# A gated linear attention and an MLP on one core: shared-memory work reordered, one cumulative sum per block, w_in in four pieces

## The chip, the core and the metric

The kernel runs on one core of a Trainium2 chip. The core has five instruction streams that run side by side and wait for each other by semaphores: TensorE (PE, matrix products into the accumulator memory PSUM), VectorE (DVE), ScalarE (ACT), GpSimd (POOL) and SyncE (SP), which here only issues data transfers. GpSimd issues transfers too. VectorE, ScalarE and GpSimd work on SBUF, the on-chip memory; VectorE and ScalarE can read PSUM as well. The metric is the device time of one execution in microseconds (us); lower is better.

## The reference: what is computed

```python
f = 1.0 / (1.0 + np.exp(-f_logit))              # q, k, v, f_logit: (4, 8, 768, 48)
for t in range(S):
    state = f[:, :, t, :, None] * state + np.einsum('bhd,bhe->bhde', k[:, :, t], v[:, :, t])
    y[:, :, t] = np.einsum('bhd,bhde->bhe', q[:, :, t], state)
x = y.transpose(0, 2, 1, 3).reshape(3072, 384)
h = x @ w_in                                     # w_in: (384, 2048)
g = 0.5 * (h + np.sqrt(h * h + 4.0))
out = g @ w_out                                  # w_out: (2048, 384)
```

A recurrent attention with a gate per key channel is followed by a two-layer MLP over all 3072 tokens.

## The kernel before

The 3072 tokens are cut into 12 blocks `p` of 256 tokens, three to a batch entry. A block stands on 128 partitions with two neighbouring tokens to a partition, and its two halves of 64 partitions are two chunks of 128 tokens. Within a chunk the recurrence is done as masked matrix products; from chunk to chunk a state of 48x48 per head is carried.

Each block goes through small named pieces. `lf`, `lq`, `lk`, `lv` load the inputs (SyncE). `ex` takes exp(-f) (ScalarE), `ut` adds 1 and gives tile `UT` (line L182), `tt` multiplies the two tokens' gates (L136), `ln` takes the logarithm, tile `s`. `hi` and `lo` split `s` into two 16-bit parts in tile `hl` (L133, L207). `cu` sums `s` over time by TensorE: two triangular matrices `tri`, each times `hi` and `lo` (L221), and small sums over an indicator matrix (L226). `ep` and `ea` are exp of the one sum and of minus the other (ScalarE, L235). `qu`, `ku` multiply q and k by the gates (L136), `qm`, `km` multiply those by `ea`, `ep` into the 16-bit tile `qk` (L136, two instructions each), `vc` casts v. `ge`, `gs`, `gb` are small decay factors. `tp`/`te` transpose `qk` by TensorE for blocks 0 to 3 (L310); `tx` does it by a DMA transpose for the later blocks. `sc` is the score product (L334), `pm` masks it (L341, reads PSUM), `yt` and `yn` give y (L391, L400), `kv`, `ia`, `sa`, `sb` carry the state (L353, L364, L371, L378). `yc` copies y, `xp`/`xe` or a DMA transpose `xx` turn it into tile `xT`.

The MLP of a block is eight pieces `m1` of six products each (L440), eight `sq` (square, ScalarE, L449), four `rt` (square root, ScalarE, L455), eight `gt` (VectorE, L465, reads PSUM), eight `m2` of four products each (L477), two `ev` (copy out) and the stores `st`. `wi0` to `wi7` load and cast w_in in eight pieces of 256 columns, `wo0` to `wo7` w_out, all issued by GpSimd in its own stream.

The order of all pieces is written out by hand in the string `ORDER`, one word each: `ut0.0:P` is piece `ut` of block 0, part 0, on P = GpSimd (D = VectorE, A = ScalarE, S = SyncE, T = TensorE with its PSUM banks behind @). Block 0 is done in two halves of four heads. Each engine runs its pieces strictly in this order, so a piece that waits holds back all behind it on its engine. `TABLE:e` and `TABLE:s` load ScalarE's function tables (exp and log, or square root). `DEPTH` says how many buffers a tile name has.

Of the kernel before, what the change touches and what calls it, by code (L numbers as in the profile page):

```python
# [47 lines left out]
tt7.0:D ln6.0:A lq6.0:S yt3:T@37 sa3:D ln7.0:A st0.01.1:S m2.1.12:T TABLE:s rt2.0:A vc4.0:D km5.0:P ia3.1:T yn3.1:T m2.1.13:T
sb3:D tx4.0:S yc3.0:D m1.2.3:T@2 yc3.1:D xp3.0:T@1 qm5.0:P m1.2.5:T@3 ev1.1:A xe3.0:D tx4.1:S sq2.3:A gt2.1:D m1.2.4:T@7
lv5.0:S rt2.1:A gt2.0:D xp3.1:T@6 m1.2.6:T@1 hi7.0:P xe3.1:D sq2.5:A kv4:T@50 lq7.0:S gt2.2:D hi6.0:P ia4.0:T sq2.4:A qu6.0:P  # L50
m1.2.7:T@6 gt2.3:D rt2.2:A m2.2.10:T@4 st0.01.0:S sa4:D gb5:P gs5:D m2.2.11:T sq2.6:A gt2.5:D ia4.1:T sq2.7:A m1.3.0:T@2
# [559 lines left out]
```

## Time and profile before

| what | value |
|---|---|
| time, median of 3 runs | 220.79 us (220.07 to 221.23) |
| the profiled execution | 221.5 us, of which 219.7 us lie between first and last instruction (the span) |
| PE busy | 183.4 us, 83% of the span |
| DVE busy | 162.9 us, 74% |
| ACT busy | 155.3 us, 71% |
| POOL busy | 118.4 us, 54% |
| mean granted TensorE clock | 0.966 of full speed |

Busy is the time in which an engine runs an instruction; for VectorE and GpSimd that includes time in which an instruction has begun but does not get on. A chain is the sequence of work that ended last, followed back from the end, at each step to what released it. The row groups below are copied from such views.

### The profile page before, as it was taken

The numbers are of one execution on the slowest core, as the hardware profiler recorded it, in microseconds if no ns is written. First come the engines' busy times: TensorE is split into PE (matmuls) and PEld (weight loads), VectorE is DVE, ScalarE is ACT, GpSimd is POOL, SyncE is SP. The second block draws the span as 40 slices with busy tenths as digits, with TensorE's granted clock in tenths as the row PEclk, the third lists the DMA queues.
The fourth block names the chain that finished last, engine by engine and source line by source line (L and its number), as shares of the span: only waits on it lengthen the run. The fifth ranks groups of instructions, "written<-read, shape, count | busy, mean of one in ns | idle before, by whom it ended". The sixth has DMA issues, their size and how long they took to land.

```text
span 219.7 us, 5661 instructions
## 1 busy us (share of the span) xinstructions
PE 183.4 (83%) x2320; PEld 130.2 (59%) x2320; DVE 162.9 (74%) x284; ACT 155.3 (71%) x252; POOL 118.4 (54%) x128
## 2 busy tenths in 40 slices
PE   0348948869589999976995799999989999999991
PEld 0225626646357776745763358678666787777760
DVE  6889685898569999959975976879557875463650
ACT  4633684979747899859994376798848859887920
POOL 6899477299975966889999902939000000000002
PEclk9999996999999999999999658999999999999998
DMA  6999999089980989999969797981991017102204
GB/s 167 267 261 248 215 267 191 8 178 214 250 188 1 206 178 282 182 238 255 174 141 142 151 141 198 184 167 29 186 126 39 0 39 144 38 1 72 75 19 125
DMA packets 82073, 32.87 MB, mean 150 GB/s; under 512 B 73952, under 2 KB 82000, under 8 KB 82048
## 3 DMA queue, kind: packets, MB, share of 16 engines
q1 hardware_dynamic: 76528, 29.07, 65.5%
q0 software_dynamic: 5520, 3.44, 10.5%
q8 instruction: 18, 0.29, 0.5%
q14 instruction: 7, 0.06, 0.1%
HBM read 25.17 MB, written 4.72 MB: 136 GB/s over the span
## 4 chain that ended last, share of the span: by engine, by line
PE 44%; DVE 15%; POOL 12%; ACT 11%; DMA 10%; issue 4%; SPq 2%; POOLq 0%; DVEq 0%
PE ps L440 18%; PE ps L477 18%; POOL UT L182 6%; DMA wout<-in_moe_w_out_dram 4%; ACT r L455 3%; DMA win<-in_moe_w_in_dram 3%; DVE qk L136 3%; DVE UT L136 3%; DVE q L136 3%; ACT hsq L449 3%; DMA qkT<-qk 2%; PE ps L334 2%; DVE pm L341 2%; POOL wout L145 2%; ACT f L175 2%
## 5 line engine op out<-in xcount | busy, mean ns | idle before, releaser
L440 PE MATMUL ps<-xT,win 128*128 128x256 f16 x576 | 75.3, 282 | 7.0 <-DVE g L465 3.2
L465 DVE SCALAR_TENSOR_TENSOR g<-ps,r 128x512 f16<-128x512 f32 x96 | 62.2, 683 | 20.8 <-ACT r L455 20.6
L477 PE MATMUL ps<-wout,g 128*128 128x384 f16 x384 | 72.4, 330 | 2.8 <-DMA wout<-in_moe_w_out_dram 2.7
L440 PEld LDWEIGHTS <-win 128*128 128x128 f16 x576 | 56.7, 101 | 19.9 <-DMA win<-in_moe_w_in_dram 4.8
L449 ACT ACTIVATE hsq<-ps 128x512 f16<-128x512 f32 x96 | 53.9, 595 | 19.0 <-PE ps L440 18.3
L455 ACT ACTIVATE r<-hsq 128x1024 f16<-128x1024 f16 x48 | 50.6, 1058 | 1.4 <-DVE g L465 0.3
L477 PEld LDWEIGHTS <-g 128*128 128x128 f16 x384 | 36.7, 99 | 24.1 <-issue 4.5
L341 DVE TENSOR_TENSOR pm<-ps,mask 128x512 f16<-128x512 f32 x48 | 30.9, 680 | 8.2 <-PE ps L334 8.2
L497 POOL DMA_DIRECT2D out_dram<-os x3 | 1.7, 568 | 61.1 <-DVE os L133 60.4
L182 POOL TENSOR_SCALAR UT<-f 128x768 f32<-128x768 f32 (+1 forms) x10 | 21.3, 2132 | 8.0 <-ACT f L175 4.6
L136 POOL TENSOR_TENSOR k<-k,UT 128x768 f32<-128x768 f32 (+1 forms) x12 | 21.1, 1763 | 2.6 <-DVE g L465 2.6
L221 PE MATMUL ps<-hl,tri 128*128 128x384 f16 (+1 forms) x52 | 12.2, 349 | 9.9 <-POOL hl L133 6.5
L133 POOL CAST v<-v 128x768 f16<-128x768 f32 (+1 forms) x10 | 8.6, 864 | 15.9 <-DMA v<-in_v_dram 15.9
L136 POOL TENSOR_TENSOR qk<-q,ea 128x384 f16<-128x384 f32 (+1 forms) x16 | 15.7, 1005 | 0.2
L334 PE MATMUL ps<-qkT 48*64 48x128 f16 x384 | 10.6, 235 | 4.0 <-DVE sn L378 1.2
L221 PEld LDWEIGHTS <-tri 128*128 128x128 f16 x52 | 5.2, 104 | 13.7 <-issue 5.4
L175 ACT ACTIVATE f<-f 128x768 f32<-128x768 f32 (+1 forms) x13 | 10.4, 798 | 3.6 <-DMA f<-in_f_logit_dram 3.6
L136 DVE TENSOR_TENSOR UT<-UT 128x384 f32<-128x384 f32 (+1 forms) x10 | 7.7, 782 | 6.8 <-POOL UT L182 6.6
L196 ACT ACTIVATE s<-UT 128x384 f32<-128x384 f32 (+1 forms) x13 | 6.5, 499 | 8.3 <-DVE UT L136 8.3
L136 POOL TENSOR_TENSOR qk<-k,ep 128x384 f16<-128x384 f32 x12 | 12.0, 1023 | 0.0
L334 PEld LDWEIGHTS <-qkT 48*64 48x64 f16 x384 | 6.9, 114 | 8.2 <-issue 5.0
L136 DVE TENSOR_TENSOR qk<-k,ep 128x384 f16<-128x384 f32 (+1 forms) x14 | 10.8, 809 | 0.8 <-issue 0.8
(69 smaller groups left out, 211.0 us busy)
## 6 DMA issues: line engine op xcount, KB each, us to landing
f<-in_f_logit_dram SPq DMA_DIRECT2D x11, 384.0 KB, 5.3
q<-in_q_dram SPq DMA_DIRECT2D x11, 384.0 KB, 5.4
k<-in_k_dram SPq DMA_DIRECT2D x11, 384.0 KB, 5.4
...
```

Of the source, the lines that this page charges most:

```text
L133: eng(e).tensor_copy(out=o, in_=i)
L136: eng(e).tensor_tensor(out=o, in0=a, in1=b, op=ALU.mult)
L175: nc.scalar.activation(out=t, in_=t, func=AF.Exp, scale=-1.0)
L182: eng(e).tensor_scalar(out=T["UT", p][:, 0::2, hs], in0=T["f", p][:, hs].rearrange("p h i d -> p i h d"), scalar1=1.0, scalar2=None, op0=A ...
L221: nc.tensor.matmul(out=o, lhsT=K["tri"][:, m], rhs=hl[:, r, hs, 0:D], start=(r == 0), stop=(r == 1))
L334: nc.tensor.matmul(out=T["sc", p, i, h][64 * cc:64 * cc + 64, j, :], lhsT=t[r, 1, j, i, :], rhs=t[r, 0, j], start=True, stop=True)
L341: nc.vector.tensor_tensor(out=T["pm", p, i, h], in0=T["sc", p, i, h], in1=K["mask"][:, i].unsqueeze(1).broadcast_to([128, 4, 128]), op=ALU ...
L440: nc.tensor.matmul(out=T["h", p, m][:, a], lhsT=K["win"][m][:, j, a * 128:(a + 1) * 128], rhs=T["xT", p][:, :, j, :], start=(j == 0), stop ...
L449: nc.scalar.activation(out=T["hsq", p, r][:, a], in_=T["h", p, m].rearrange("p a c t -> p (a c t)"), func=AF.Square, scale=1.0)
L455: nc.scalar.activation(out=T["r16", p, r], in_=T["hsq", p, r], func=AF.Sqrt, scale=0.25, bias=1.0)
L465: nc.vector.scalar_tensor_tensor(out=T["g", p][:, 2 * m:2 * m + 2, :].rearrange("p a t -> p (a t)"), in0=T["h", p, m].rearrange("p a c t - ...
L477: nc.tensor.matmul(out=T["o", p, cc], lhsT=T["g", p][:, jn, cc * 128:(cc + 1) * 128], rhs=K["wout"][jn // 2][:, jn % 2, :], start=(jn == 0 ...
```

## The change

All words of `ORDER` are rewritten: pieces change their place and some their engine. Apart from the order:

- `ut` runs on VectorE alone (before: nine full blocks and half of block 0 on GpSimd). `tt`, `hi`, `lo`, `km`, `qm` go the other way: VectorE has 4 full `tt` instead of 8, no `hi` and no `lo` instead of 4 and 6, one full `km` instead of 5 and one full `qm` instead of 4. `qu` on VectorE: 5 instead of 2. Nothing in the code makes VectorE and GpSimd wait for each other where they did not before; only the order and the engines are other.
- Blocks 3 to 11 (`ADD1`) sum with one triangular matrix instead of two; a new piece `c1` on VectorE adds `s` to that sum (reads PSUM and SBUF, writes tile `ea`), and `ea` takes the exp in place.
- Block 0 (`DIRECT`) has no `hi`/`lo`: its `s` goes in 32 bits straight into the products.
- w_in is loaded in four pieces of 512 columns instead of eight of 256.
- `UT`, `hsq` and `r16` have three buffers instead of two. ScalarE loads its tables 12 times instead of 10, copies y 8 times instead of 13, VectorE 16 instead of 11.

```diff
+DIRECT = [0]
+ADD1 = [3, 4, 5, 6, 7, 8, 9, 10, 11]
...
-DEPTH = {'f': 3, 'q': 3, 'k': 3, 'v': 3, 'UT': 2, 's': 2, 'ep': 2, 'ea': 2, 'v16': 4, 'ge': 3, 'gs': 4, 'gb': 3, 'qkT0': 2, 'qkT1': 2, 'pm00': 2, 'pm01': 2, 'pm10': 2, 'pm11': 2, 'sn0': 2, 'sn1': 2, 'y16': 2, 'xT': 5, 'hsq': 2, 'r16': 2, 'g': 4, 'os': 2}
+DEPTH = {'f': 3, 'q': 3, 'k': 3, 'v': 3, 'UT': 3, 's': 2, 'ep': 2, 'ea': 2, 'v16': 4, 'ge': 3, 'gs': 4, 'gb': 3, 'qkT0': 2, 'qkT1': 2, 'pm00': 2, 'pm01': 2, 'pm10': 2, 'pm11': 2, 'sn0': 2, 'sn1': 2, 'y16': 2, 'xT': 5, 'hsq': 3, 'r16': 3, 'g': 4, 'os': 2}
...
-lf0.0:S lf0.1:S lf1.0:S lk0.1:S lk0.0:S TABLE:e ex0.0:A lq0.1:S ut0.0:P ex0.1:A lq0.0:S tt0.0:D ut0.1:D ln0.0:A lf2.0:S
-tt0.1:D hi0.0:P ln0.1:A lo0.0:D ex1.0:A hi0.1:P cu0.0:T@01 lo0.1:P lq1.0:S ut1.0:D ku0.1:P cu0.1:T@01 lv0.1:S tt1.0:D ea0.1:A
...
+lf0.1:S lf0.0:S lf1.0:S lk0.0:S lk0.1:S TABLE:e ex0.1:A lq0.1:S ut0.1:D ex0.0:A tt0.1:D lq0.0:S ut0.0:D lf2.0:S tt0.0:P
+ex1.0:A lv0.1:S ku0.0:D ln0.0:A lv0.0:S ln0.1:A cu0.0:T@01 ut1.0:D cu0.1:T@01 ku0.1:D ep0.0:A qu0.1:P lk1.0:S ea0.0:A tt1.0:D
...
+    for i in range(4):
+        def win(e, b, i=i):
+            nc.gpsimd.dma_start(out=K["win"][i], in_=moe_w_in[:, i * 512:(i + 1) * 512].rearrange("(j p) n -> p j n", p=128))
+        W.add(f"wi{i}", "P", win, makes=[f"win{i}"], dma=("w", 2.37), cost={"P": 0.83})
...
-        def win(e, b, i=i):
-            nc.gpsimd.dma_start(out=K["win"][i], in_=moe_w_in[:, i * 256:(i + 1) * 256].rearrange("(j p) n -> p j n", p=128))
...
-            W.add(f"ut{p}.{x}", "DP", ut, reads=[f"e{p}.{x}"], makes=[f"u{p}.{x}"], uses=[("f", p), ("UT", p)],
-                  cost={"D": 0.07 + 2 * n / 960 , "P": 0.19 + 0.86e-3 * 2 * n})
+            W.add(f"ut{p}.{x}", "D", ut, reads=[f"e{p}.{x}"], makes=[f"u{p}.{x}"], uses=[("f", p), ("UT", p)],
+                  lock=True, cost={"D": 0.05 + 0.83e-3 * 2 * n})
...
+                if p in DIRECT:
+                    nc.scalar.activation(out=K["s32"][:, hs, 0:D], in_=T["UT", p][:, 1, hs], func=AF.Ln)
+                    return
...
+            mats = [0] if p in ADD1 else [0, 1]
...
+                if p in DIRECT:
+                    tri, ind, terms = K["tri32"], K["ind32"], [K["s32"]]
+                else:
+                    hl = K["hl"][p % NHL]
+                    tri, ind, terms = K["tri"], K["ind"], [hl[:, 0], hl[:, 1]]
+                for m in mats:
                     o = T["cum", p, m][:, h0 * D:h1 * D]
-                    for r in range(2):
-                        nc.tensor.matmul(out=o, lhsT=K["tri"][:, m], rhs=hl[:, r, hs, 0:D], start=(r == 0), stop=(r == 1))
+                    for r, t in enumerate(terms):
+                        nc.tensor.matmul(out=o, lhsT=tri[:, m], rhs=t[:, hs, 0:D], start=(r == 0), stop=(r == len(terms) - 1))
...
+            if p in ADD1:
+                def c1(e, bk, x=x, hs=hs, h0=h0, h1=h1, p=p):
+                    if ("ea", p) not in T:
+                        T["ea", p] = sb("ea", p, [128, 8, 48], FP32)
+                    nc.vector.tensor_tensor(out=T["ea", p][:, hs], in0=T["cum", p, 0][:, h0 * D:h1 * D].rearrange("p (h d) -> p h d", d=D),
+                                            in1=T["s", p][:, hs], op=ALU.add)
+                W.add(f"c1{p}.{x}", "D", c1, reads=[f"cum{p}.{x}", f"s{p}.{x}"], makes=[f"cumi{p}.{x}"],
+                      uses=[("ea", p), ("s", p), ("bank", f"cx{p}")], cost={"D": 0.15 + 1.05e-3 * n})
...
-                W.add(f"{nm}{p}.{x}", "A", xp, reads=[f"cum{p}.{x}"], makes=[f"{nm}{p}.{x}"],
-                      uses=[(nm, p), ("bank", f"c{'x1'[m]}{p}")], table="e", cost={"A": 0.17 + 0.85e-3 * n})
+                    t = T[nm, p][:, hs].rearrange("p h d -> p (h d)")
+                    nc.scalar.activation(out=t, in_=t if m == 1 and p in ADD1 else T["cum", p, m][:, h0 * D:h1 * D], func=AF.Exp, scale=sgn)
...
-                        nc.tensor.matmul(out=T["h", p, m][:, a], lhsT=K["win"][m][:, j, a * 128:(a + 1) * 128],
+                        nc.tensor.matmul(out=T["h", p, m][:, a], lhsT=K["win"][m // 2][:, j, m % 2 * 256 + a * 128:m % 2 * 256 + a * 128 + 128],
...
+    s32 = konst.tile([128, 8, 64], FP32, name="s32")
+    nc.vector.memset(s32[:, :, D:64], 0.0)
+    tri32 = konst.tile([128, 2, 128], FP32, name="tri32")
+    nc.vector.tensor_copy(out=tri32, in_=tri)
+    ind32 = konst.tile([128, 3], FP32, name="ind32")
+    nc.vector.tensor_copy(out=ind32, in_=ind)
...
-    win = [konst.tile([128, 3, 256], FP16, name=f"win{i}") for i in range(8)]
+    win = [konst.tile([128, 3, 512], FP16, name=f"win{i}") for i in range(4)]
```

What stands on GpSimd while w_in is loaded: before, from piece 1 to piece 7 (`win` is a piece of w_in, `k<-k,UT` is `ku`, `gb` a decay factor, `UT<-f` is `ut`, `hl<-s` is `hi`, `v<-v` is `vc`).

```order
L142 DMA win_114<-in_moe_w_in_dram 128x3x256
L142 DMA win_115<-in_moe_w_in_dram 128x3x256
L136 TENSOR_TENSOR k<-k,UT 128x2x8x48
L142 DMA win_117<-in_moe_w_in_dram 128x3x256
L136 TENSOR_TENSOR gb<-gs,ge 128x8
L142 DMA win_116<-in_moe_w_in_dram 128x3x256
L182 TENSOR_SCALAR UT<-f 128x2x384
L142 DMA win_118<-in_moe_w_in_dram 128x3x256
L133 CAST hl_92<-s 128x8x48
L142 DMA win_119<-in_moe_w_in_dram 128x3x256
L133 CAST v_557<-v 128x768
L142 DMA win_120<-in_moe_w_in_dram 128x3x256
```

And now, from the first piece of w_in to the last, on the same engine (`qk<-k,ep` is `km`, `UT<-UT` is `tt`, `hl<-s,hl` is `lo`).

```order
L144 DMA win_119<-in_moe_w_in_dram 128x3x512
L135 CAST hl_91<-s 128x8x48
L138 TENSOR_TENSOR gs<-ge,half 128x24
L214 TENSOR_TENSOR hl_91<-s,hl_91 128x8x48
L138 TENSOR_TENSOR qk_96<-k,ep 128x4x2x48 x2
L138 TENSOR_TENSOR gb<-gs,ge 128x8
L144 DMA win_120<-in_moe_w_in_dram 128x3x512
L144 DMA win_121<-in_moe_w_in_dram 128x3x512
L138 TENSOR_TENSOR UT<-UT 128x384
L149 DMA wout_126<-in_moe_w_out_dram 128x2x384
L144 DMA win_122<-in_moe_w_in_dram 128x3x512
```

Ahead of the last piece stand no `ut` and no `ku` any more; a `lo`, a `km`, a `tt` and one piece of w_out do.

VectorE around the gates of the last blocks, before: `tt` and small work of blocks 8 to 11 (`sn` is the state, `qk<-k,ep` is `km` of block 9).

```order
L136 TENSOR_TENSOR UT<-UT 128x384
L133 CAST hl_91<-s 128x8x48
L136 TENSOR_TENSOR gs<-ge,half 128x24
L207 TENSOR_TENSOR hl_91<-s,hl_91 128x8x48
L371 TENSOR_TENSOR sn_2275<-ps_2236,gs 128x384
L136 TENSOR_TENSOR gs<-ge,half 128x24
L207 TENSOR_TENSOR hl_92<-s,hl_92 128x8x48
L136 TENSOR_TENSOR qk_95<-k,ep 128x4x2x48 x2
L378 TENSOR_TENSOR sn_2325<-ps_2237,gb 128x384
L136 TENSOR_TENSOR qk_95<-q,ea 128x4x2x48 x2
```

And now, on VectorE at the gates of the same blocks (`ea<-ps,s` is the new `c1` of blocks 8 and 9, `UT<-f` is `ut` of blocks 11 and 10, `g` the MLP's `gt`).

```order
L495 SCALAR_TENSOR_TENSOR g<-ps_1944,r_1975 128x512
L495 SCALAR_TENSOR_TENSOR g<-ps_1977,r_2029 128x512
L252 TENSOR_TENSOR ea<-ps_2018,s 128x384
L495 SCALAR_TENSOR_TENSOR g<-ps_1966,r_2029 128x512
L252 TENSOR_TENSOR ea<-ps_2050,s 128x384
L408 TENSOR_TENSOR sn_2090<-ps_1997,gb 128x384
L185 TENSOR_SCALAR UT<-f 128x2x384 x2
L371 TENSOR_TENSOR pm_2152<-ps_2104,mask 128x512
L371 TENSOR_TENSOR pm_2161<-ps_2105,mask 128x512
L371 TENSOR_TENSOR pm_2172<-ps_2128,mask 128x512
L371 TENSOR_TENSOR pm_2181<-ps_2129,mask 128x512
L135 COPY os<-ps_2035 128x384
```

The two-input work on SBUF (`UT<-UT`, `hl<-s,hl`, `qk<-k,ep`) has left this stretch for GpSimd; `c1` and two `ut` stand between steps that read PSUM.

TensorE's cumulative sum of block 4, before (two PSUM tiles, `hi` and `lo` for each, then the small sums).

```order
L221 LDWEIGHTS tri
L221 MATMUL ps_994<-hl_91,tri 128x384
L221 LDWEIGHTS tri
L221 MATMUL ps_994<-hl_91,tri 128x384
L221 LDWEIGHTS tri
L221 MATMUL ps_995<-hl_91,tri 128x384
L221 LDWEIGHTS tri
L221 MATMUL ps_995<-hl_91,tri 128x384
L226 LDWEIGHTS hl_91
```

And now the same block: one PSUM tile, two products fewer.

```order
L234 LDWEIGHTS tri
L234 MATMUL ps_1035<-hl_91,tri 128x384
L234 LDWEIGHTS tri
L234 MATMUL ps_1035<-hl_91,tri 128x384
L239 LDWEIGHTS hl_91
```

## Rows read from the trace of the kernel before

**Rows 1.** The page: span, then busy us (share) and instructions of each engine.

```profile
span 219.7 us, 5661 instructions
PE 183.4 (83%) x2320; PEld 130.2 (59%) x2320; DVE 162.9 (74%) x284; ACT 155.3 (71%) x252; POOL 118.4 (54%) x128
```

**Rows 2.** Windows: us, busy (count) of each engine, TensorE clock, DMA share, GB/s.

```profile
24.21:60.47 36.26, 27.20 (x336) 18.56 (x337) 27.80 (x47) 28.26 (x44) 29.21 (x29) 0.95 0.99 188
60.47:131.48 71.01, 62.92 (x876) 43.45 (x876) 60.67 (x96) 52.97 (x89) 55.38 (x52) 0.94 0.92 174
131.48:213.14 81.66, 80.59 (x916) 59.67 (x915) 54.12 (x90) 62.27 (x95) 13.56 (x14) 0.99 0.45 89
```

**Rows 3.** Chain that ended last, late part: start us, us, what (count).

```profile
196.15 3.93 PE ps L440 x36
206.60 6.51 PE ps L477 x40
```

**Rows 4.** The same chain, TensorE's attention work between 106 and 114 us.

```profile
106.95 0.45 PE ps L353 x16
107.40 0.40 PE ps L391 x32
...
111.67 0.65 PE ps L221 x4
112.32 0.18 PE ps L226 x8
112.50 0.63 PE ps L334 x32
```

**Rows 5.** The same chain where it runs over weight loads.

```profile
31.31 6.53 DMA win<-in_moe_w_in_dram
...
52.56 7.87 DMA wout<-in_moe_w_out_dram
```

**Rows 6.** The same chain before the first MLP product.

```profile
8.10 1.18 DVE UT L136
...
15.83 2.31 DVE q L136
```

**Rows 7.** VectorE's groups by shape: count, busy us, mean ns, idle before.

```profile
L136 DVE TENSOR_TENSOR qk<-k,ep 128x384 f16<-128x384 f32 x10 | 8.8, 915 | 0.8 <-issue 0.8
L136 DVE TENSOR_TENSOR UT<-UT 128x384 f32<-128x384 f32 x8 | 7.0, 888 | 6.1 <-POOL UT L182 5.9
L371 DVE TENSOR_TENSOR sn<-ps,gs 128x384 f16<-128x384 f32 x12 | 6.6, 550 | 2.4 <-PE ps L353 1.2 <-PE ps L364 1.2
...
L207 DVE TENSOR_TENSOR hl<-s,hl 128x384 f16<-128x384 f32 x6 | 5.0, 826 | 0.0
...
L136 DVE TENSOR_TENSOR q<-q,UT 128x384 f32<-128x384 f32 x2 | 4.2, 2100 | 0.0
...
L136 DVE TENSOR_TENSOR gs<-ge,half 128x24 f32<-128x24 f32 x6 | 2.8, 469 | 0.0
```

**Rows 8.** VectorE in order of time: start us, us, instruction, count.

```profile
121.99 0.55 DVE L207 TENSOR_TENSOR hl<-s,hl 128x384 f16<-128x384 f32 x1
122.46 3.43 DVE L136 TENSOR_TENSOR qk<-k,ep 128x384 f16<-128x384 f32 x2
...
126.28 1.01 DVE L136 TENSOR_TENSOR qk<-q,ea 128x384 f16<-128x384 f32 x2
```

**Rows 9.** GpSimd in order of time, two stretches.

```profile
68.43 2.50 POOL L182 TENSOR_SCALAR UT<-f 128x768 f32<-128x768 f32 x1 [3.68 <-ACT f L175]
...
121.03 2.36 POOL L136 TENSOR_TENSOR qk<-q,ea 128x384 f16<-128x384 f32 x2
123.35 2.12 POOL L136 TENSOR_TENSOR k<-k,UT 128x768 f32<-128x768 f32 x1
```

**Rows 10.** VectorE in order of time at 69.7 us.

```profile
69.71 0.55 DVE L182 TENSOR_SCALAR UT<-f 128x768 f32<-128x768 f32 x1
```

**Rows 11.** Line L182 (`ut`): duration ns min/median/max, first and last start us, shapes.

```profile
L182 POOL TENSOR_SCALAR UT<-f x10: 1177/2134/2499, 4.0 to 115.6; 128x768 f32<-128x768 f32 x9, 128x384 f32<-128x384 f32 x1
...
L182 DVE TENSOR_SCALAR UT<-f x3: 355/546/691, 5.5 to 69.7; 128x768 f32<-128x768 f32 x2, 128x384 f32<-128x384 f32 x1
```

**Rows 12.** Tile `win`: GpSimd's issues of w_in, and their time to landing.

```profile
L142 POOL DMA_DIRECT2D win<-in_moe_w_in_dram x8: 762/794/983, 14.1 to 31.3; - x8
...
DMA to landing us min/median/max: 6.2/6.7/8.2
```

**Rows 13.** Waits: who waited for whom, us in total, times, longest us.

```profile
DVE g L465 <- ACT r L455: 20.6, 25, 3.1
...
POOL v L133 <- DMA v<-in_v_dram: 15.9, 3, 9.7
```

More of the change, by code (lines that the diff above doesn't have):

```diff
@@ L48 @@
[L48 to L51, printed above, removed]
-gt2.4:D lf8.0:S rt2.3:A m1.3.1:T@5 sb4:D vc5.0:P sc4.1:T@37 sq3.0:A gt2.7:D lo6.0:P m1.3.3:T@0 lk7.0:S sq3.1:A lv8.0:S
@@ L196, in ln @@
                 nc.scalar.activation(out=T["s", p][:, hs], in_=T["UT", p][:, 1, hs], func=AF.Ln)
-            W.add(f"ln{p}.{x}", "A", ln, reads=[f"t{p}.{x}"], makes=[f"s{p}.{x}"], uses=[("UT", p), ("s", p)], table="e",
+            W.add(f"ln{p}.{x}", "A", ln, reads=[f"t{p}.{x}"], makes=[f"s{p}.{x}"], uses=[("UT", p), ("s32", p) if p in DIRECT else ("s", p)], table="e",
                   cost={"A": 0.2 + 0.85e-3 * n})
-            def hi(e, bk, x=x, hs=hs, p=p):
-                copy(e, K["hl"][p % NHL][:, 0, hs, 0:D], T["s", p][:, hs])
@@ L224, in cu @@
                     for j in range(4):
-                        for r in range(2):
-                            nc.tensor.matmul(out=nl[:, j], lhsT=hl[:, r, 2 * j:2 * j + 2, :], rhs=K["ind"],
-                                             start=(r == 0), stop=(r == 1))
-            W.add(f"cu{p}.{x}", "T", cu, reads=[f"{w}{p}.{y}" for w in ("lo", "hi") for y in (xs if last else [x])], makes=[f"cum{p}.{x}"], uses=[("hl", p)],
-                  banks=[f"cx{p}", f"c1{p}"], mode="F", cost={"T": 0.67 * nh / 8 + (0.24 if last else 0.0)})
+                        for r, t in enumerate(terms):
+                            nc.tensor.matmul(out=nl[:, j], lhsT=t[:, 2 * j:2 * j + 2, :], rhs=ind,
+                                             start=(r == 0), stop=(r == len(terms) - 1))
+            need = xs if last else [x]
+            sides = [f"s{p}.{y}" for y in need] if p in DIRECT else [f"{w}{p}.{y}" for w in ("lo", "hi") for y in need]
+            full = 0.67 if p not in DIRECT else 1.4
+            W.add(f"cu{p}.{x}", "T", cu, reads=sides, makes=[f"cum{p}.{x}"], uses=[("s32", p) if p in DIRECT else ("hl", p)],
+                  banks=[f"cx{p}"] + ([] if p in ADD1 else [f"c1{p}"]), mode="F",
+                  cost={"T": full * len(mats) / 2 * nh / 8 + ((0.24 if p not in DIRECT else 0.5) if last else 0.0)})
+            if p in ADD1:
[6 more added lines that the diff above has]
+                      uses=[("ea", p), ("s", p), ("bank", f"cx{p}")], cost={"D": 0.15 + 1.05e-3 * n})
             for m, nm, sgn in ((0, "ep", 1.0), (1, "ea", -1.0)):
@@ L234, in xp @@
                         T[nm, p] = sb(nm, p, [128, 8, 48], FP32)
-                    nc.scalar.activation(out=T[nm, p][:, hs].rearrange("p h d -> p (h d)"),
-                                         in_=T["cum", p, m][:, h0 * D:h1 * D], func=AF.Exp, scale=sgn)
-                W.add(f"{nm}{p}.{x}", "A", xp, reads=[f"cum{p}.{x}"], makes=[f"{nm}{p}.{x}"],
-                      uses=[(nm, p), ("bank", f"c{'x1'[m]}{p}")], table="e", cost={"A": 0.17 + 0.85e-3 * n})
+                    t = T[nm, p][:, hs].rearrange("p h d -> p (h d)")
+                    nc.scalar.activation(out=t, in_=t if m == 1 and p in ADD1 else T["cum", p, m][:, h0 * D:h1 * D], func=AF.Exp, scale=sgn)
+                if m == 1 and p in ADD1:
+                    W.add(f"{nm}{p}.{x}", "A", xp, reads=[f"cumi{p}.{x}"], makes=[f"{nm}{p}.{x}"], uses=[(nm, p)], table="e",
+                          cost={"A": 0.2 + 0.85e-3 * n})
+                else:
+                    W.add(f"{nm}{p}.{x}", "A", xp, reads=[f"cum{p}.{x}"], makes=[f"{nm}{p}.{x}"],
+                          uses=[(nm, p), ("bank", f"c{'x1'[m]}{p}")], table="e", cost={"A": 0.17 + 0.85e-3 * n})
             def qu(e, bk, x=x, hs=hs, p=p):
@@ L279, in gs @@
                 K["half"].unsqueeze(1).unsqueeze(1).broadcast_to([128, 3, 4, 2]))
-        W.add(f"gs{p}", "DP", gs, reads=[f"ge{p}"], makes=[f"gs{p}"], uses=[("ge", p), ("gs", p)], cost={"D": 0.2, "P": 0.25})
+        W.add(f"gs{p}", "DP", gs, reads=[f"ge{p}"], makes=[f"gs{p}"], uses=[("ge", p), ("gs", p)], lock=True, cost={"D": 0.2, "P": 0.22})
         if not first:
@@ L567, in ps @@
         return psp.tile(shape, dt, name=f"ps{bank}", tag=f"ps{bank}", bufs=1)
-    K = {"hl": hl, "qk": qk, "tri": tri, "ind": ind, "half": half, "ident": ident, "mask": mask, "win": win, "wout": wout}
+    K = {"s32": s32, "tri32": tri32, "ind32": ind32, "hl": hl, "qk": qk, "tri": tri, "ind": ind, "half": half, "ident": ident, "mask": mask, "win": win, "wout": wout}
     W = Work()
```

179 lines of the change are left out of this document (92 added, 87 removed).

## The prediction

> **What bounds the kernel now.** I read the page first: no engine is full, TensorE with 183.4 of 219.7 us is nearest [rows 1]. Busy is not need, though, so the second step is what TensorE needs when nothing holds it. Late in the chain 36 first-layer products run in 3.93 us and 40 second-layer products in 6.51 [rows 3], 0.109 and 0.163 each: 576 and 384 of them make 62.9 and 62.5. The attention's products, at the chain's prices [rows 4]: 384 for scores 7.6, 384 for y 4.8, 192 for the state 5.4, 44 whole and 8 half ones for the cumulative sums 7.8, 96 small sums 2.2, together 27.8; the kinds without a row (carry, query times state, transposes) I put at about 11 at the same price per column. TensorE needs about 164 us of the 219.7. The other 55 are what a change of order can win, and the windows say where they lie [rows 2]:
>
> - up to 24.21, where the first MLP product starts: about 6.5 needed, 17.7 not;
> - 24.21 to 60.47: 16 `m1` (10.5), 7 `m2` (4.6) and some 7 of attention, 22 of 36.3; 14 not needed;
> - 60.47 to 131.48: what remains of the 164 is 56 of 71.0; 15 not needed;
> - 131.48 to 213.14: 80.6 busy of 81.7, hardly 2 to win;
> - the last 6.6: copy and store.
>
> In the second stretch the chain runs over weight loads: the last piece of w_in, 6.53 from 31.31 on, and the last of w_out, 7.87 from 52.56 on [rows 5]. GpSimd issues them in order behind its elementwise work. In the first and third the chain runs over VectorE. The two products of `km` take 1.01 undisturbed, but 3.43 at 122.46, ending at 125.89, 0.4 after the end of the second of two GpSimd instructions that overlap them [rows 8, 9]. A two-input instruction on SBUF takes 0.55 alone [rows 8]; the groups average 888 ns for `tt`, 915 for `km`, 826 for `lo`, 2100 for `qu` [rows 7]. Over 0.55 (0.505 for a half of `km`) that is 2.7 + 4.1 + 1.7 + 3.1 = 11.6 us of VectorE time spent behind GpSimd. What reads PSUM isn't touched: `sa` stays at 550 ns over 12 [rows 7].
>
> **The change, part by part.** *Lead-in.* Before the first MLP product the chain holds a `tt` of 1.18 and a `qu` of 2.31 [rows 6]; against 0.55 they lose 0.6 and 1.8, and stretched pieces between them some 1.5. Their GpSimd neighbours are gone from there, so up to 3.9 comes back. Against it, block 0's sums in 32 bits have no row. They replace eight half-width 16-bit products (0.65 in all) by four; if one costs as much as a 16-bit one 0.33 is won, if four times as much 0.65 is lost, and if its weight load is not hidden nearly 1 more. I take the loss of 0.65, nearer to the two passes that a 16-bit pair already needs, and another 1.2 for block 0's `ln`, which now stands behind block 1's `ex`. Lead-in: -2 (bounds -3.9 to +1). The Trainium skill, FP8 and Floating Point Precision, TensorE Precision Notes, has true 32-bit products take four passes, which no run here shows; by it the sum is the one taken.
>
> *w_in.* Four issues of 0.79 [rows 12] fall away. The last piece stands behind a `tt` that waits for VectorE's `ut` of block 3, just ahead of the copies that start the MLP; with the lead-in above that is near 22.2, and `tt` (about 1), one w_out issue and its own (0.8 each) bring the end of the issue to about 24.8, against 32.1. A piece takes 6.7 to land [rows 12] and now holds twice the bytes: at best no longer (31.5), at worst twice as long (38.2); I take 1.2 to 2 us more, landing near 33 instead of 37.8. w_out's last piece has about 4.5 us less GpSimd work ahead of it (four `ut` at 2.13 [rows 11] and the four issues off, `lo`, `km`, `qm` and casts on). Second stretch: -5 (bounds -7 to +1).
>
> *Gates and contention.* A `ut` takes 2.13 on GpSimd and 0.55 on VectorE [rows 11], so the first link of each gate chain is 1.6 shorter in nine blocks. VectorE gains nine `ut` (4.9), nine `c1` (one PSUM input, as `sa`: 0.55 each, 5.0), three `qu` and five copies of y (4.4); it loses four `tt`, six `lo`, four `hi`, four `km`, three `qm` (about 14). Its own undisturbed work is the same; what it wins is the 11.6 of waiting, if the new order keeps the pairs apart in fact. VectorE is idle for 18.8 of the 107.3 us of the two middle stretches [rows 2], which covers single additions; without that cover each `c1` costs 0.55 between sum and `ea`. I take half of the third stretch's 15: -7.5 (bounds 0, all of it spent otherwise, and -13.5).
>
> *TensorE.* Nine blocks lose two products of 0.163: -2.9, in full once TensorE is what ends last, nothing where it still waits.
>
> *ScalarE.* Two more table loads are covered by five fewer copies of y and by 19.4 us of idle time in the last stretch [rows 2].
>
> *Late stretch.* Blocks 10 and 11 take their sums some 13 us of TensorE work later than before (after `m1` of block 6, before after the first `m1` of block 5). Behind those sums GpSimd has about 13.5 us (two `ku`, two `km`, two `qm`, a `qu`, a cast) and the transposes follow, while TensorE has some 21 of other work before block 10's scores. Tight: +2.5 (bounds 0 to +8).
>
> Sum: -2 - 5 - 7.5 - 2.9 + 2.5 = -14.9, a span of 204.8 and a profiled execution of 206.6 instead of 221.5. The profiled one lies 0.7 above the median, so 206.
>
> **A rule weighed.** GpSimd's `ut` of 68.43 to 70.93 takes 2.50 instead of 2.13, and VectorE's own `ut` starts inside it and takes its ordinary 0.55 [rows 9 to 11]: GpSimd gave way by 0.37. By this row nine `ut` on VectorE cost GpSimd 3.3 us, which its idle time hides, and VectorE nothing. The Trainium skill, SBUF — State Buffer, Who interferes with whom, says otherwise: a one-input VectorE instruction in a two-port mode and GpSimd hold the shared ports exclusively, and the later one stands until the other is done. By that rule VectorE would have waited about 1.2 us here, and it did not; but `km` at 122.46 behaves as the rule says. What it would make of the sum is the second rival.
>
> **Rivals.** *1. Late blocks arrive too late.* GpSimd waits 15.9 us for v in three waits, once 9.7 [rows 13]; now the casts of v for blocks 9 and 8 stand ahead of `ku` and `qu` of 11. A wait of 9.7 there goes on to `qm` and the scores of blocks 10 and 11: 206 + 9.7 - 2.5 = 213. Against it: v of block 9 is issued earlier in SyncE's order. Chance 0.12.
>
> *2. The moved `ut` waits for GpSimd.* Order alone keeps the pair apart, no semaphore does. If each of nine starts inside a GpSimd instruction and stands half of a typical 2.1, 9.5 us come back: 215. For it: the `km` row; against it: the `ut` row. Chance 0.08.
>
> *3. Slower: VectorE's queue holds the chains.* All eighteen `ut` and `c1` stand between `gt` steps that wait for the square root, 20.6 us in 25 waits [rows 13], 0.82 each. If each of the eighteen inherits such a wait and with its own 0.55 lands on TensorE's path, 18 x 1.37 = 24.7 is added: 231. It decides from 0.83 us per instruction on, 14.9 over 18. Against it: VectorE's 18.8 idle and a third buffer for `UT`, `hsq` and `r16`. Chance 0.06.
>
> *4. No change.* The pieces of w_in land at 38, TensorE starves as before, and drift brings the contention back: only the 2.9 and noise are left, 218 to 221. Chance 0.06.
>
> **How the numbers follow.** The forecast (198 to 212) has 0.64, something better than 198 has 0.04. The likeliest is 206. The range reaches over the first two rivals to 217; better than 198, the slower rival and no change lie outside, with 0.16 between them. What a measurement of this kernel tells from no change is about 0.5%, the spread of its runs. Faster by more: forecast, the better case, rivals 1 and 2 and a little of 4: 0.89. Slower: rival 3 and a little of 4: 0.06. The rest, 0.05, is the same.
>
> **What the profile will show.** `tt`, `km`, `lo` and `qu` on VectorE near 0.55 (0.505 for a half of `km`), not 0.9 to 2.1, show the contention gone; `c1` at 0.55 and untouched by GpSimd shows its price; the first MLP product near 22 and the last piece of w_in landed by 33 show the first two terms; TensorE dense from about 55 on, and 2,300 less 18 products at unchanged prices, the third and fourth. `ut` on VectorE over 1 us speaks for rival 2; long idle time before `c1` or `ut` with `gt` just ahead for rival 3; a gap of TensorE at the scores of blocks 9 to 11 for rival 1. The prediction is wrong if TensorE still idles 10 us or more between 60 and 130.

## The result, and the profile after

| | before | after |
|---|---|---|
| time, median | 220.43 us (219.66 to 221.23, 4 runs) | 205.93 us (205.34 to 208.38, 4 runs) |
| ratio after to before, 95% interval | | 0.936 (0.928 to 0.945) |
| profiled execution, span | 221.5, 219.7 | 205.34, 203.6 |

The changed kernel is 14.5 us faster; 206.0 was predicted. The total is right, two of its terms are not. Ratios leave disturbed executions out; the profiles of `b_win4` and `best2` are such, so none of their rows is shown.

The page of the changed kernel, as [rows 1]:

```profile
span 203.6 us, 5630 instructions
PE 177.7 (87%) x2302; PEld 129.1 (63%) x2302; DVE 147.3 (72%) x285; ACT 154.9 (76%) x248; POOL 108.6 (53%) x135
```

VectorE is busy 15.6 us less and GpSimd 9.8 less, though nine `ut` and nine `c1` came to VectorE. Where the time came from is read from the windows, cut as in [rows 2]: first MLP product, last of w_out landed, and some 910 TensorE products left.

```profile
26.11:56.36 30.25, 26.52 (x418) 19.77 (x415) 26.07 (x48) 29.08 (x45) 27.94 (x32) 0.97 1.14 223
56.36:114.55 58.19, 56.72 (x775) 40.88 (x775) 48.94 (x87) 50.40 (x80) 48.53 (x57) 1.00 0.92 194
114.55:197.00 82.45, 78.57 (x912) 56.87 (x911) 54.47 (x94) 61.55 (x94) 18.89 (x21) 0.98 0.51 93
```

| stretch | before | after | moved | predicted |
|---|---|---|---|---|
| to the first MLP product | 24.21 | 26.11 | +1.9 | -2 |
| w_in and w_out arrive | 36.26 | 30.25 | -6.0 | -5 |
| middle | 71.01 | 58.19 | -12.8 | -7.5, and of -2.9 a part |
| late | 81.66 | 82.45 | +0.8 | +2.5, and the rest of -2.9 |

The last 6.6 are as before. The cuts do not hold the same work: the second stretch now has 418 products instead of 336, the middle 775 instead of 876, so part of the middle's 12.8 is work done earlier. TensorE's idle time tells more: it falls from 9.1 to 3.7 in the second stretch and from 8.1 to 1.5 in the middle, and grows from 1.1 to 3.9 in the late one.

Another part of the middle is TensorE's clock. Before, the granted clock fell to the lower level at 122, after a wait of 2.28 us for VectorE's `hl` and one of 0.53, and six first-layer products took 1.44 us instead of 0.82. From the kernel before:

```profile
122.20:131.48 9.28, 8.02 (x77) 4.26 (x76) 7.97 (x11) 5.21 (x10) 3.75 (x3) 0.54 0.79 116
123.51 1.44 PE L440 MATMUL ps<-xT,win 128*128 128x256 f16 x6
...
135.43 0.82 PE L440 MATMUL ps<-xT,win 128*128 128x256 f16 x6
```

At the ratio of these two rows the 8.0 busy us hold some 3 us (an estimate) that the changed kernel, with 1.00 throughout its middle, does not spend. VectorE's groups by shape, as [rows 7], say why TensorE waits less:

```profile
L185 DVE TENSOR_SCALAR UT<-f 128x768 f32<-128x768 f32 x11 | 6.3, 590 | 0.4 <-POOL v L135 0.4
L252 DVE TENSOR_TENSOR ea<-ps,s 128x384 f32<-128x384 f32 x9 | 4.9, 547 | 0.6 <-ACT ep L262 0.6
L138 DVE TENSOR_TENSOR q<-q,UT 128x384 f32<-128x384 f32 x5 | 3.2, 633 | 2.5 <-DMA q<-in_q_dram 2.5
L138 DVE TENSOR_TENSOR UT<-UT 128x384 f32<-128x384 f32 x4 | 2.2, 558 | 0.0
...
L138 DVE TENSOR_TENSOR qk<-k,ep 128x384 f16<-128x384 f32 x2 | 1.0, 548 | 0.0
```

`tt` fell from 888 to 558 ns, `km` from 915 to 548, `qu` from 2100 to 633; `c1` (`ea<-ps,s`) costs the expected 0.55 and `ut` 0.59. No semaphore keeps the two engines apart, only the order and the choice of engine: there are 4 `tt` where there were 8, and 2 instructions of `km` where there were 10.

The lead-in went the other way. TensorE in order of time, its start, duration and, in brackets, the idle time before it; first two rows of the kernel before, the end of block 0's sums and of its scores:

```profile
8.13 0.40 PE L226 MATMUL ps<-ind,hl 128*128 128x3 f16 x8
...
18.04 0.64 PE L334 MATMUL ps<-qkT 48*64 48x128 f16 x16
```

And the changed kernel:

```profile
7.46 2.93 PE L234 MATMUL ps<-s,tri 128*128 128x192 f32 x8 [7.46 <-ACT s L198]
10.18 1.31 PE L239 MATMUL ps<-ind,s 128*128 128x3 f32 x8
...
17.17 1.46 PE L234 MATMUL ps<-hl,tri 128*128 128x384 f16 x4
...
19.88 0.82 PE L383 MATMUL ps<-v,qk 64*128 64x96 f16 x16 [1.05 <-ACT v L133]
20.64 1.46 PE L234 MATMUL ps<-hl,tri 128*128 128x384 f16 x4
...
22.23 0.82 PE L421 MATMUL ps<-v,pm 64*128 64x48 f16 x32
...
26.11 0.61 PE L470 MATMUL ps<-xT,win 128*128 128x256 f16 x2
```

Block 0's 32-bit sums end at 11.49, 3.0 later than before. Both block 0's scores and block 1's sums (which stood among those scores before and stand behind them now) are done at 18.83, against 18.68 before: 2.8 of the 3.0 have come back, since the stretched VectorE pieces are gone, as predicted. Then 2.6 are lost: 1.05 for a cast of v that stands behind other ScalarE work, and 1.6 for block 2's sums (at 20.64), which now stand ahead of block 0's y (`v,pm`). Behind y 0.9 comes back.

w_in, as [rows 12]; the last issue begins at 26.3 and is the slowest to land, at 36.7 instead of 37.8 (33 predicted):

```profile
L144 POOL DMA_DIRECT2D win<-in_moe_w_in_dram x4: 762/776/949, 15.1 to 26.3; - x4
...
DMA to landing us min/median/max: 6.0/7.5/10.4
```

The late blocks show the first rival in a small form. Waits, as [rows 13]:

```profile
POOL qk L138 <- DVE q L138: 4.7, 2, 4.5
PE ps L470 <- DMA xT<-y: 3.5, 2, 2.0
DVE q L138 <- DMA q<-in_q_dram: 2.7, 2, 2.5
```

q of block 9 came late; VectorE's `qu` waited 2.5 for it and GpSimd's `qm` 4.5 for `qu`. TensorE waited 2.0 for y of block 7, which `a_late` below shows to be mostly another matter.

### The profile page after: what moved, and what is told of

The parts are those of the page before. It is cut to its first block, busy times and chain, and to the rows that moved or that the text cites. A ratio compares the mean times of both kernels' runs of the same rounds, so it can differ in the third digit from the quotient of the medians.

```text
span 203.6 us, 5630 instructions
## 1 busy us (share of the span) xinstructions
PE 177.7 (87%) x2302; PEld 129.1 (63%) x2302; DVE 147.3 (72%) x285; ACT 154.9 (76%) x248; POOL 108.6 (53%) x135
## 4 chain that ended last, share of the span: by engine, by line
issue 32%; PE 26%; POOL 18%; DMA 15%; ACT 3%; DVE 2%; SPq 2%; POOLq 0%
PE ps L507 10%; POOL qk L138 6%; PE ps L470 6%; DMA q<-in_q_dram 4%; PE ps L234 4%; POOL k L138 4%; DMA xT<-y 3%; DMA wout<-in_moe_w_out_dram 3%; DMA v<-in_v_dram 2%; POOL wout L149 2%; DMA f<-in_f_logit_dram 2%; POOL v L135 2%; POOL hl L214 2%; PE ps L364 1%; PE ps L383 1%
## 5 line engine op out<-in xcount | busy, mean ns | idle before, releaser
L138 POOL TENSOR_TENSOR qk<-q,ea 128x384 f16<-128x384 f32 x20 | 19.9, 1014 | 4.7 <-DVE q L138 4.7
L138 POOL TENSOR_TENSOR qk<-k,ep 128x384 f16<-128x384 f32 x20 | 19.8, 1013 | 0.3 <-ACT ge L302 0.2
L138 POOL TENSOR_TENSOR k<-k,UT 128x768 f32<-128x768 f32 x10 | 18.1, 1815 | 1.7 <-DMA k<-in_k_dram 1.6
L178 ACT ACTIVATE f<-f 128x768 f32<-128x768 f32 (+1 forms) x13 | 10.3, 795 | 3.3 <-DMA f<-in_f_logit_dram 3.2
L138 POOL TENSOR_TENSOR UT<-UT 128x384 f32<-128x384 f32 (+1 forms) x8 | 7.8, 984 | 8.9 <-DVE UT L185 8.9
L214 POOL TENSOR_TENSOR hl<-s,hl 128x384 f16<-128x384 f32 x11 | 10.0, 912 | 4.8 <-ACT hl L133 4.7
L133 ACT COPY os<-ps 128x384 f32<-128x384 f32 x12 | 5.8, 480 | 8.6 <-PE ps L507 7.2
L401 DVE TENSOR_TENSOR sn<-ps,gs 128x384 f16<-128x384 f32 x12 | 6.6, 554 | 7.7 <-PE ps L383 5.3
L135 POOL CAST v<-v 128x768 f16<-128x768 f32 x10 | 8.2, 821 | 5.2 <-DMA v<-in_v_dram 5.2
L135 DVE COPY os<-ps 128x384 f32<-128x384 f32 x12 | 6.5, 552 | 4.8 <-PE ps L507 3.1
L262 ACT ACTIVATE ep<-ps 128x384 f32<-128x384 f32 (+1 forms) x13 | 6.0, 470 | 5.2 <-PE ps L239 5.0
```

The source lines that it names most:

```text
L135: eng(e).tensor_copy(out=o, in_=i)
L178: nc.scalar.activation(out=t, in_=t, func=AF.Exp, scale=-1.0)
L214: eng(e).tensor_tensor(out=hl[:, 1, hs, 0:D], in0=T["s", p][:, hs], in1=hl[:, 0, hs, 0:D], op=ALU.subtract)
```

## Experiments

The theory after the result: the middle stretch was won because both elementwise queues got shorter, VectorE's by the waiting behind GpSimd, GpSimd's by `ut`. Rivals: fewer TensorE products; shorter gate chains rather than shorter queues; fewer issues of w_in. Each time stands beside the kernel before in the same session; "later than the changed kernel" compares medians with its 205.93, and by the intervals such a difference is uncertain by 2 to 3 us.

**`b_add1`: one cumulative sum, alone, on the kernel before.**

```diff
+ADD1 = [3, 4, 5, 6, 7, 8, 9, 10, 11]
-m1.1.0:T@4 ea3.0:A ut4.0:P
+m1.1.0:T@4 c13.0:D ea3.0:A ut4.0:P
```

> The kernel before with one part of the change alone: blocks 3 to 11 sum with one triangular matrix, and VectorE's c1 makes the second sum, right ahead of ea (blocks 9 and 10: ahead of ep). Order and engines are otherwise those of before, c1 and contention included. Theory (a product saved counts only where TensorE ends last): nearly all these sums stand in stretches where TensorE of before still waits, so it gives 0 to -1, and nine c1 on a contended VectorE may cost 0 to 2: 219.5 to 222. Rival (the term of the prediction counts in full wherever it stands): 217.5.

Measured: 223.91 against 219.67, ratio 1.019 (1.011 to 1.028). Slower by 1 to 3%, more than either expectation allowed. TensorE is busy 3.2 us less and the end is later all the same. What the trace shows is ScalarE waiting for the new piece, 14.9 us in eight waits, where the changed kernel has one of 1.2; that this is the whole loss is not shown.

```profile
ACT ea L261 <- DVE ea L251: 7.7, 6, 2.0
ACT ep L261 <- DVE ea L251: 7.2, 2, 4.5
```

**`b_win4`: four pieces of w_in, alone, on the kernel before.**

```diff
-wi1:P vc0.0:A pm0.11:D ea1.0:A kv0:T@23 wi2:P
+vc0.0:A pm0.11:D ea1.0:A kv0:T@23 wi1:P
```

> The kernel before with w_in in four pieces alone, each issued where the first of its two old pieces that is used was issued (pieces 0, 2, 4 and 6 of before). Theory (the issues were in the way of GpSimd, 0.8 each): the last piece lands 1 to 2 us earlier than 37.8 and the end is 0 to 1.5 earlier, 219 to 220.5. Rival (the bytes set the landing, and a bigger piece lands later): last piece at 37 to 39 and the end as before or up to 1 later, 220 to 222.

Measured: 220.35 against 219.67, ratio 1.001 (0.997 to 1.006), no change. The pieces alone are worth nothing.

**`a_win8`: eight pieces again, on the changed kernel.**

```diff
-wi1:P
+wi2:P wi3:P
```

> The changed kernel with w_in in eight pieces of 256 columns again, two issues at the place of each of the four. Theory (the number of issues is a side matter, the place in GpSimd's queue and the bytes per us set when w_in is there): last piece landed at 36.5 to 38, first eight first-layer pieces and the end within 1 of the changed kernel. Rival (the four issues of 0.8 less are what moved w_in forward): 2 to 4 later, 208 to 210.

Measured: 208.35 against 220.19, ratio 0.948 (0.942 to 0.954); the last piece landed at 38.8, the middle starts 2.1 later. The median is 2.4 later than the changed kernel's, as the rival had it: in this order, where the issues stand together, four more cost about 2. The intervals of the two kernels just overlap, so the size is not certain.

**`a_utP`: `ut` of blocks 3 to 11 back on GpSimd, on the changed kernel.**

```diff
-ut5.0:D
+ut5.0:P
```

> The changed kernel with ut of blocks 3 to 11 back on GpSimd, at the same places. Theory (gates and contention are the larger part of what was won): each gate chain gets 1.6 longer again, GpSimd gets 19 us more work and some of it lies over VectorE's SBUF work again; 4 to 10 are lost, 210 to 216, with VectorE's tt, qu and km again over 0.6. Rival (the order alone, and the fewer TensorE products, made the gain, and GpSimd's idle time hides the nine ut): within 1 of the changed kernel, 205 to 207.

Measured: 218.09 against 219.67, ratio 0.995 (0.990 to 0.999). Nearly the whole gain is lost, more than the theory gave, and its second part fails in the main: little contention comes back with it. VectorE's `tt`, GpSimd's `ut`, and the window of the middle:

```profile
L137 DVE TENSOR_TENSOR UT<-UT 128x384 f32<-128x384 f32 x4 | 2.2, 562 | 4.8 <-POOL UT L184 4.7
L184 POOL TENSOR_SCALAR UT<-f 128x768 f32<-128x768 f32 x9 | 19.5, 2169 | 1.5 <-ACT f L177 1.4
60.92:127.00 66.08, 58.31 (x778) 41.51 (x776) 46.50 (x82) 51.21 (x85) 61.19 (x64) 1.00 0.82 170
```

`tt` stays at 562 ns; the two `km` take 794 and the five `qu` 711, 0.9 us more in all than in the changed kernel. But GpSimd is busy 61.2 of 66.1 us: it is now the fullest engine, ahead of TensorE with 58.3.

**`a_pool9`: is it the queue or the gate chain?** Nine idle fills in GpSimd's queue, with the real `ut` left on VectorE.

```diff
+        def zz(e, bk, i=i):
+            nc.gpsimd.tensor_scalar(out=K["zz"][:, 1], in0=K["zz"][:, 0], scalar1=1.0, scalar2=None, op0=ALU.add)
-ut5.0:D
+zz5:P ut5.0:D
```

> The changed kernel with nine idle fills on GpSimd, each with the shape that ut has there (2.1 to 2.2 us), in the places of GpSimd's own queue where ut of blocks 3 to 11 would stand; the real ut stays on VectorE, so that no gate chain has a longer link. Theory (putting ut on GpSimd cost 12.2 because it fills GpSimd's queue, whose pieces the scores and first-layer products wait for): 8 to 13 later, 214 to 219. Rival (it cost that because each gate's own chain got 1.6 longer, and GpSimd's idle time would have covered the work): 0 to 4 later, 206 to 210.

Measured: 217.34 against 220.19, ratio 0.990 (0.984 to 0.995), 11.4 later than the changed kernel. Most of it is the queue, with one reservation in the rows: beside the fills VectorE's `ut` takes 905 ns instead of 590, 3.5 in all.

```profile
L154 POOL TENSOR_SCALAR zz<-zz 128x768 f32<-128x768 f32 x9 | 20.1, 2236 | 0.2
L189 DVE TENSOR_SCALAR UT<-f 128x768 f32<-128x768 f32 x11 | 9.8, 905 | 1.4 <-ACT f L182 0.6 <-POOL zz L154 0.4 <-POOL q L137 0.4
61.35:126.00 64.65, 59.73 (x777) 42.24 (x775) 51.45 (x88) 51.05 (x84) 61.00 (x63) 0.97 0.82 174
```

**`b_utD`: the other way round, all ten `ut` to VectorE on the kernel before.**

```diff
-ut5.0:P
+ut5.0:D
```

> The kernel before with nothing changed but the engine of ut: all ten that GpSimd does go to VectorE, at the same places in the order. Theory now (GpSimd's queue was what the middle stretches waited for, and ut, 2.13 each there, is the largest single thing in it; VectorE's waiting behind GpSimd is a side matter): 4 to 9 are won, 211 to 216, though VectorE's tt, km, lo and qu stay over 0.8. Rival (the place of ut pays only together with the new order): within 1.5 of before, 218.5 to 221.

Measured: 211.96 against 219.69, ratio 0.966 (0.957 to 0.974). Ten letters in the order give 7.7, half of the gain, with most of the contention still there; by the prediction's sum 7.8 of the 11.6 us are left (with `lo` at 781 and `qu` at 614 ns), and `ut` itself is now stretched by 2.2:

```profile
L181 DVE TENSOR_SCALAR UT<-f 128x768 f32<-128x768 f32 x11 | 8.3, 751 | 1.7 <-ACT f L174 1.6
L135 DVE TENSOR_TENSOR qk<-k,ep 128x384 f16<-128x384 f32 x10 | 7.7, 807 | 0.6 <-ACT ge L271 0.4 <-issue 0.2
L135 DVE TENSOR_TENSOR UT<-UT 128x384 f32<-128x384 f32 x8 | 7.5, 952 | 0.1
```

**`a_vec11`: what VectorE's waiting is worth.** Eleven idle fills on VectorE, on the changed kernel.

```diff
+            nc.vector.memset(K["zz"][:, 0:1056], 0.0)
-ut5.0:D
+zz0:D ut5.0:D
```

> The changed kernel with eleven idle fills of a spare SBUF tile on VectorE, about 1 us each, ahead of ut of blocks 5 to 11, tt8, km3, qu3 and qu5: it gives VectorE back the 11.6 us that its SBUF work spent behind GpSimd before, without touching any order or GpSimd's queue. The prediction's theory (that waiting is worth about half its time): 4 to 7 later, 210 to 213. Rival (VectorE's idle time covers it, the waiting was not on the path): 0 to 2 later, 206 to 208.

Measured: 214.16 against 219.69, ratio 0.978 (0.968 to 0.988), 8.2 later for 10.3 us of fills. The middle grows by 6.2:

```profile
L154 DVE MEMSET zz<- 128x1056 f32 x11 | 10.3, 938 | 1.8 <-DVE UT L189 0.5 <-issue 0.3 <-ACT hsq L483 0.2
60.10:124.50 64.40, 60.16 (x778) 42.08 (x776) 55.45 (x96) 50.95 (x82) 53.34 (x58) 0.97 0.84 174
```

VectorE's time is on the path too, and at 0.8 us lost per us it looks like more than the half that the prediction took. But the fills also stretch GpSimd's work beside them, whose busy time grows by 4.1: `gs` takes 410 ns instead of 259.

```profile
L137 POOL TENSOR_TENSOR gs<-ge,half 128x24 f32<-128x24 f32 x9 | 3.7, 410 | 0.0
```

If the costs of the two queues simply add up, this run (9.3 us of busy time more on VectorE, 4.1 on GpSimd) and `a_pool9` (4.0 and 20.0) together give some 0.7 us per us on VectorE and 0.4 on GpSimd, an estimate from two medians.

**`a_sum2`: the two products back, on the changed kernel.** Blocks 3 to 11 also multiply by the second matrix; that result is overwritten.

```diff
-                for m in mats:
-                    o = T["cum", p, m][:, h0 * D:h1 * D]
+                for m in more + mats:
+                    o = T["cum", p, m if m in mats else 0][:, h0 * D:h1 * D]
```

> The changed kernel with the two products of the second triangular matrix put back in blocks 3 to 11; their result is overwritten by the first sum's, and c1 stays. Theory (TensorE is what ends last in the changed kernel from 26 on): the whole 18 x 0.163 = 2.9 comes back, 208.3 to 209.3. Rival (TensorE still waits often enough to hide them): within 1 of the changed kernel.

Measured: 207.25 against 219.69, ratio 0.947 (0.937 to 0.956). By the medians 1.3 comes back, by the ratios 2.2; the intervals overlap, so neither the 2.9 nor nothing is excluded.

**`a_hilo0`: block 0 in two 16-bit parts, on the changed kernel.**

```diff
-DIRECT = [0]
+DIRECT = []
-ln0.0:A lv0.0:S ln0.1:A cu0.0:T@01
+ln0.0:A hi0.0:D lo0.0:D lv0.0:S ln0.1:A hi0.1:D lo0.1:D cu0.0:T@01
```

> The changed kernel with block 0 split into two 16-bit parts again, hi and lo of both halves on VectorE right behind ln. Theory (the 32-bit sums cost some 2 us of the lead-in, and TensorE is dense behind it): the sums end near 10 instead of 11.5, the first MLP product starts near 24.5 instead of 26.1, the end is 1 to 1.6 earlier: 204.3 to 205. Rival (the last piece of w_in, landing at 36.7, holds the eight first-layer pieces anyway): first product earlier, the wait for w_in longer by the same, the end unchanged within 0.4.

Measured: 207.14 against 219.67, ratio 0.944 (0.938 to 0.950), not faster than the changed kernel. TensorE:

```profile
8.07 1.67 PE L233 MATMUL ps<-hl,tri 128*128 128x192 f16 x8 [8.07 <-DVE hl L134]
9.54 0.40 PE L238 MATMUL ps<-ind,hl 128*128 128x3 f16 x8
...
25.54 0.82 PE L469 MATMUL ps<-xT,win 128*128 128x256 f16 x3
```

The sums take 1.87 instead of 4.03 and end 1.55 earlier, but the first MLP product gains 0.6 and the end nothing (its median is 1.2 later, which the intervals do not separate): the last piece of w_in still lands at 36.6, which speaks for the rival.

**`best1`: the whole front rearranged.** It also lost the explicit table loads behind the front, so that ScalarE loads 18 times instead of 12, six loads (7.7 us) that no expectation named.

```diff
-sc0.0:T@45 tt2.0:D sc0.1:T@67 cu1.0:T@10 ku1.0:D ln2.0:A vc0.1:A
+wi1:P sc0.0:T@45 ut2.0:D tt2.0:D sc0.1:T@67 vc0.1:A vc0.0:A cu1.0:T@10
...
-cu2.0:T@41 pm0.11:D lk2.0:S sa0:D yt0:T@60
+lk2.0:S km1.0:P sa0:D yt0:T@60 gs1:D yn0.1:T cu2.0:T@41
```

> The changed kernel with the front rearranged: block 0 in two 16-bit parts on VectorE, q of block 0 loaded ahead of f of block 1, tt of block 1 on GpSimd, the mask products ahead of block 1's ku, block 2's sums behind block 0's y, w_in's pieces spread between the first GpSimd pieces (last issue ahead of gb2 instead of behind tt3), and q of block 9 loaded ahead of q of block 10. Theory (what stands ahead of the first MLP product is lost one to one, and w_in must come earlier with it): first product at 22.5 to 23.5, last piece of w_in landed by 32, the end 2 to 3 earlier than 205.9: 202.5 to 204. Rival (loads of the later blocks, pushed back by the earlier w_in, or the waits at 130 to 160 eat it): 205 to 207.

Measured: 206.08 against 219.69, ratio 0.941 (0.934 to 0.947), no gain. First product at 24.18, later than the 22.5 to 23.5 expected, and w_in at 31.0; then block 1's state product waits 5.15 for GpSimd's cast of v. By the chain (first row) this goes back to k of block 2, 15 us under way, whose `ku` and `km` stand ahead of that cast; v itself landed at 32.4. Late, block 11's state product waits for an output buffer, and what follows is slow:

```profile
15.29 15.03 DMA k<-in_k_dram
...
35.04 0.82 PE L381 MATMUL ps<-v,qk 64*128 64x96 f16 x16 [5.15 <-POOL v L133]
...
157.29 0.52 PE L381 MATMUL ps<-v,qk 64*128 64x96 f16 x16 [1.99 <-ACT os L131]
...
159.33 1.48 PE L468 MATMUL ps<-xT,win 128*128 128x256 f16 x6
```

**`best2`: the same front, with that put right.**

```diff
-lf4.0:S
+lv1.0:S
...
-lq2.0:S
+lk2.0:S
...
-lk2.0:S
+lq2.0:S
...
-lv1.0:S
+lf4.0:S
...
-TABLE:e ep3.0:A
+TABLE:e ex4.0:A ep3.0:A
```

> The rearranged front again (two 16-bit parts for block 0, earlier w_in), now with what the last one ran into put right: ScalarE's 12 table loads where the changed kernel has them, v of block 1 and k of block 2 loaded ahead of q of block 2, f of blocks 4 and 5 loaded and used later, and block 5's second store ahead of block 6's stores. Theory (the state product of block 1 waited 5.2 for v, that of block 11 2.0 for an output buffer): both waits under 1, m1 of block 1 at 39.5 to 41, the end 3 to 6 earlier than the changed kernel: 200 to 203. Rival (the bytes needed before 36 are fixed, so another load is late instead): 204.5 to 206.5.

Measured: 202.33 against 220.19, ratio 0.919 (0.913 to 0.924), inside the theory's 200 to 203. It has the two moves of the next run in it (one since `best1`), so what the front alone gives is not shown.

**`a_late`: two transfers moved in SyncE's queue, on the changed kernel.**

```diff
-lq10.0:S
+lq9.0:S lq10.0:S
...
-lq9.0:S
...
-st5.01.0:S
+st5.01.0:S st5.01.1:S
...
-st5.01.1:S
```

> The changed kernel with two transfers moved in SyncE's queue and nothing else: q of block 9 ahead of q of block 10 (in the changed kernel GpSimd waited 4.5 for what is made from it, and TensorE 2.0 behind that), and block 5's second store ahead of block 6's stores (TensorE waited 0.8 for the output buffer). Theory (the late stretch's loss is a matter of two late transfers, the first rival in a small form): the wait ahead of the first product of block 7's MLP falls from 2.0 to about 1, the one at block 11's state product to under 0.5, the end 1 to 3 earlier: 203 to 205. Rival (the sums of blocks 10 and 11 stand too late whatever is loaded): within 0.7 of the changed kernel.

Measured: 202.67 against 220.77, ratio 0.922 (0.915 to 0.929). The waits:

```profile
PE ps L469 <- DMA xT<-y: 3.6, 2, 1.9
...
POOL qk L137 <- DVE q L137: 1.3, 2, 1.1
```

`qm`'s 4.5 became 1.1. From the run of 36 first-layer products at 112.48 (here at 115.18) to the last run of second-layer products it takes 73.5 us instead of 77.2. TensorE's waits in it fall from 3.9 to 1.7: one of 1.13 behind VectorE and block 11's of 0.76 are gone, but that ahead of block 7's MLP fell only from 2.0 to 1.7, less than expected. The rest of the gain is that the lower clock behind that wait (last section) does not occur. What each of the two moves gives is not shown. Both versions beat the changed kernel, by about 3 us each.

## Why the prediction was right in total and wrong in two terms

That 206.0 was met within 0.1 is partly luck. Up to the end of the second stretch 4.1 of the 7 us came; the middle made up for it, partly by a clock that the prediction doesn't price and partly by more than it asked of the queues.

- **Gates and contention (-7.5): right in place, half right in mechanism, too small.** With the TensorE term the middle gave 12.8, some 3 of it by the clock. TensorE idles 2.6 us between 60 and 130, where 10 was the sign of being wrong. `b_utD` gives 7.7 for `ut` alone, `a_vec11` takes 8.2 for 10.3 us of fills on VectorE. The prediction named the gate chain's link of 1.6 as `ut`'s worth; `a_pool9` shows that it is mostly GpSimd's queue, to which that term gave no price. A kernel with the contention alone put back was not tried, so its share stays an estimate.
- **Lead-in (-2): wrong sign, +1.9.** One step that failed is the price of the 32-bit sums, a loss of 0.65 on 16-bit products of 0.65 in all: products this early take double time, the small sums had no price in 32 bits, and the sums take 4.03 against 1.87, 2.2 more. But by `a_hilo0` only 0.6 of this reaches the first product; what decided, by the rows of the lead-in, is that block 2's sums and a cast of v stand ahead of block 0's y, 2.6 that the prediction did not cost. `best1`, with both moved, starts at 24.18, but it changes the front in other ways too.
- **w_in and the second stretch (-5): -6.0, by another way.** The last piece landed at 36.7, not 33: the fourth issue took 10.4 to land where about 9 was taken, and was itself made 2.2 later than predicted. The stretch is shorter because it starts 1.9 later and w_out's last piece is in at 56.36 instead of 60.47, 4.1 earlier, as the 4.5 us less of GpSimd work ahead of it had promised. The pieces were worth nothing before (`b_win4`) and about 2 in the new order (`a_win8`, not certain).
- **TensorE (-2.9): not shown in full.** Alone it is a loss (`b_add1`); put back it costs 1.3, unclear (`a_sum2`).
- **Late (+2.5): about right.** The stretch shows a net +0.8: 2.8 more idle time of TensorE and 2.0 less busy time. `a_late` wins some 3: the cause was two transfers in SyncE's queue, q of block 9 and a store, and the clock behind a wait, not v as the first rival had it.
- **The second rival (`ut` held by GpSimd)** did not happen: 0.59 each. It is real where the order doesn't prevent it: in `a_pool9`, VectorE's two `ut` here and GpSimd's `ku` and fill beside them:

```profile
83.31 2.42 DVE L189 TENSOR_SCALAR UT<-f 128x768 f32<-128x768 f32 x2 [0.64 <-ACT f L182]
...
82.40 1.81 POOL L137 TENSOR_TENSOR k<-k,UT 128x768 f32<-128x768 f32 x1 [0.89 <-DMA k<-in_k_dram]
84.19 2.43 POOL L154 TENSOR_SCALAR zz<-zz 128x768 f32<-128x768 f32 x1
```

The first `ut` takes 1.32, the 0.55 of its work from about the end of `ku` on; the second, inside the fill, 1.17, and it ends 0.9 before the fill does. The rule of the Trainium skill (SBUF — State Buffer, Who interferes with whom) holds for the first, beside a two-input instruction. For the second it does not: by it `ut` would have stood until the fill's end at 86.6.
